# Turning the first half's mirrored tiles by scattered accumulation, one flip matmul for the rest, late residuals summed by transfers, and taps behind the warm-up, in a gated mix of a long convolution and an MLP

## Chip, cores, metric

One core of one Trainium2 chip. The metric is device time in microseconds (us) of one launch, median of several launches. A run counts as slow when it is over 1.5% above the fastest of the same kernel. A ratio is the mean time of one kernel's fast runs over the mean of the other's fast runs of the same rounds, so it is not quite the ratio of the medians that are quoted. Spans and starts are those of the one profiled launch of each kernel; that of the kernel before (245.66 us, granted clock 0.99) is slow, so no difference of some tenths of a us against it is read as an effect.

## The reference, cut to what matters

Shapes: 2048 rows (16 tiles of 128), D = 640, F = 1536, bfloat16.

```python
def reference(A_q, A_k, A_v, A_shift_k, A_ssm_k, A_ssm_D, B_x, B_w1, B_w2, B_w3, B_w4, gate_w):
    x = A_q
    g = sigmoid((x * gate_w).sum(-1))
    # A: 4-tap shift of k, times v, causal convolution with ssm_k over 2048 rows (by FFT), plus D, times q
    kv = (sum over 4 taps of shifted k * shift_k) * v
    y = irfft(rfft(kv, 4096) * rfft(ssm_k, 4096))[:2048] + kv * ssm_D
    a = x * y
    # B: layer norm, w1, gelu, shifts of four groups, w2, residual; layer norm, w3, gelu, w4, residual
    x1 = x + shifted(gelu(layernorm(x) @ w1)) @ w2
    b = x1 + gelu(layernorm(x1) @ w3) @ w4
    return g * a + (1 - g) * b
```

## The kernel before: what the change and the argument touch

The kernel records operations (`P.op`, `P.dma`); a list scheduler with tuned biases fixes one order for each engine, and every engine runs its list in that order. The convolution is made of transforms folded at 1024 rows: 16 final steps (k = 0 to 15; 0 to 7 are columns 0 to 319, the "first half") each turn one spectrum into two tiles of 128 rows, `ts_` and `td`. The two inverse transforms `ab[0]`, `ab[1]` give tile `ts_` as their sum and tile `td` as their difference with the rows in reverse. The reversal ("flip") is a matmul with a reversed identity. Both results are multiplied with gated rows of q and accumulated onto the output by a transfer from GpSimd (k < 12), or added to the residual and stored.

```python
    for i in range(WARM):                        # 12 pairs of warm-up matmuls
        P.op("pe", [warm-up matmul] * 2, ...)
    ...
    for c in range(DC):                          # 5 tap matmuls; the schedule puts them among the warm-ups
        pr = ps(1, "set")
        mm(pr, [(Esel[:, 128 * c:128 * (c + 1)], shk5)])
        act(SHK[:, ::-1, 128 * c:128 * (c + 1)], pr..., ACTF.Copy)

    def pool_pow(o, a, e, dur=900):              # layer norms: x ** -0.5 on GpSimd, 128 x 1 or 128 x 2 elements
        P.op("pool", lambda g: g.tensor_tensor(o, a, e, ALU.pow), [a, e], [o], dur)

    def mm4(t):                                  # w4; the residual of the second half by an identity matmul
        for h in range(2):
            mm(pr[:, h, :], [... w4 ...] + ([] if summed(h, t) else [(ident, X[:, t, hs])]))
        act(X[:, t, :]..., pr, ACTF.Copy, scale=gst[4][:, t:t + 1])
        P.dma("pool", o, x, accum=True)

    def unit(hh, c):                             # products of spectra on VectorE
        def prod(o, a, r):
            tt(v3(o), XF[:, hh, c - a], h, ALU.mult)       # 128 x 2560 as two of 1280, both inputs in SBUF
        # ... cut

    def final(hh, c, q, k):
        qt, gy, ab = qb[k], gyb[k % 8], (abb[k % 4] if k < 12 else abl[k - 12])
        P.dma(sp, qt, rows(A_q))
        act(qt[:, 0], qt[:, 0], ACTF.Copy, scale=gst[3][:, ts_:ts_ + 1])
        # ... two inverse transforms into pr
        act(ab, pr, ACTF.Copy)
        tt(gy[:, 0], ab[:, 0], ab[:, 1], ALU.add)
        mm(pf, [(flip, ab[:, 0]), (negflip, ab[:, 1])])
        act(gy[:, 1], pf, ACTF.Copy, scale=gst[3][:, td:td + 1])
        tt(gy, gy, qt, ALU.mult)                 # k >= 14: in two parts
        # k < 12: P.dma("pool", rows(out), gy, accum=True);  k >= 12: add X, store by SyncE
```

## Time and profile before

| kernel before | |
|---|---|
| time, median of 3 runs | 245.17 us (242.52 to 246.2) |
| profiled span | 243.6 us (slow) |
| busy: TensorE / VectorE / GpSimd | 228.8 / 216.6 / 95.3 us |
| matmuls; GpSimd instructions | 1486; 120 |
| TensorE's last unbroken stretch ends | 234.96 us |
| from there to the end (below: the tail) | 8.6 us |

The prediction shows the lines. In them PE is TensorE (PEld its weight loads), DVE VectorE, ACT ScalarE, POOL GpSimd and SP SyncE; SBUF and PSUM are the two on-chip memories, and matmuls write to PSUM. Only one more of the kernel before is needed later: the longest GpSimd instruction (apart from the closing drain) is a power operation of 2.0 us.

### The profile page before, as it was taken

Reading aid. Unit: us, or ns where it says so; the run is one execution under the profiler, and the core shown is the slowest. Engines: PE = TensorE matmul, PEld = TensorE weight load, DVE = VectorE, ACT = ScalarE, POOL = GpSimd, SP = SyncE. Lnnn points to the kernel's source line nnn. Section 1 sums busy time; section 2 is a strip of 40 time slices with the busy share of each in tenths; the row PEclk is TensorE's granted clock in tenths of the full one; section 3 lists DMA queues with packets and bytes.
Section 4 is the critical chain, followed back from the end, with each engine's and each line's share of the span. In section 5 each row is a group of like instructions: output and inputs, shape, how many; then the busy total and the mean of one; then the engine's idle time right before and its main releaser. Section 6 shows DMA issues by size and latency. Waiting matters only on the chain.

```text
span 243.6 us, 4130 instructions
## 1 busy us (share of the span) xinstructions
PE 228.8 (94%) x1486; PEld 136.9 (56%) x1486; DVE 216.6 (89%) x384; ACT 171.2 (70%) x317; POOL 95.3 (39%) x120
## 2 busy tenths in 40 slices
PE   6998998999997999999999999999999999999970
PEld 1276775544643654555577545775557754677640
DVE  5859999999988999999998569999999999997382
ACT  2456797888775999999375996337895466228980
POOL 0235524970272470530246321335105375323761
PEclk9999999999999999999999999999999999999996
DMA  6999599899699999489747963399987989997997
GB/s 179 348 344 341 156 224 158 202 210 241 156 189 181 295 261 269 127 202 335 206 68 152 168 164 81 64 149 193 200 208 113 164 95 169 171 176 129 128 125 137
DMA packets 65304, 45.53 MB, mean 187 GB/s; under 512 B 28930, under 2 KB 60548, under 8 KB 65284
## 3 DMA queue, kind: packets, MB, share of 16 engines
q1 hardware_dynamic: 56268, 33.36, 53.9%
q0 software_dynamic: 8832, 11.80, 33.1%
q8 instruction: 11, 0.18, 0.3%
q10 hardware_dynamic: 184, 0.11, 0.3%
q14 instruction: 9, 0.07, 0.1%
HBM read 24.29 MB, written 6.55 MB: 127 GB/s over the span
## 4 chain that ended last, share of the span: by engine, by line
PE 70%; DVE 15%; DMA 7%; POOL 3%; issue 2%; ACT 1%; DVEq 0%
PE PSall L1246 65%; DVE arena L1226 8%; DMA arena<-in_B_w_dram 4%; PE PSall L1272 4%; DMA arena<-arena 2%; POOL arena L1231 2%; DVE arena L1479 2%; DVE arena L1231 2%; DVE arena L1412 2%; ACT arena L1236 1%; POOL arena L1416 1%; DVE arena L1413 0%; PE PSall L1457 0%; DVE arena L1514 0%; DVE arena L1268 0%
## 5 line engine op out<-in xcount | busy, mean ns | idle before, releaser
L1246 PE MATMUL PSall<-arena 128*128 128x320 bf16 (+4 forms) x1420 | 217.2, 312 | 5.7 <-ACT arena L1236 2.9
L1226 DVE TENSOR_TENSOR arena<-arena 128x640 bf16<-128x640 bf16 (+5 forms) x231 | 178.5, 824 | 12.0 <-ACT arena L1236 10.7
L1246 PEld LDWEIGHTS PSall<-arena 128*128 128x128 bf16 (+1 forms) x1420 | 131.1, 98 | 90.9 <-ACT arena L1236 6.5
L1236 ACT ACTIVATE arena<-PSall 128x512 bf16<-128x512 f32 (+4 forms) x181 | 109.3, 674 | 26.6 <-PE PSall L1246 22.4
L1236 ACT ACTIVATE arena<-arena 128x640 bf16<-128x640 bf16 (+3 forms) x70 | 45.8, 692 | 12.1 <-DVE arena L1226 8.8
L240 POOL DMA_DIRECT2D out_dram<-arena x28 | 29.3, 1112 | 32.9 <-ACT arena L1236 25.6
L1231 POOL TENSOR_SCALAR arena<-arena 128x1 f32<-128x1 f32 (+2 forms) x41 | 24.7, 610 | 39.1 <-ACT arena L1236 14.2
L1236 ACT ACTIVATE arena<-PSall,arena 128x640 bf16<-128x640 f32 (+1 forms) x32 | 20.8, 660 | 25.6 <-PE PSall L1246 25.3
L1416 POOL TENSOR_TENSOR arena<-arena 128x1 f32<-128x1 f32 (+1 forms) x24 | 20.6, 877 | 44.4 <-DVE arena L1231 43.9
L240 POOL DMA_DIRECT2D arena<-arena x12 | 14.9, 1238 | 26.2 <-DVE arena L1226 25.7
L1231 DVE TENSOR_SCALAR arena<-arena 128x640 bf16<-128x640 bf16 (+3 forms) x47 | 14.3, 317 | 3.0 <-ACT arena L1236 1.4
L1412 DVE BATCH_NORM_STATS2 arena<-arena 128x6 f32<-128x320 bf16 x32 | 13.9, 476 | 2.5 <-DMA arena<-in_A_q_dram 2.4
L1272 PE MATMUL PSall<-arena 128*128 128x512 bf16 x24 | 9.7, 566 | 2.3 <-DVE arena L1268 2.3
L1479 DVE TENSOR_SCALAR arena<-arena 32x256 bf16<-32x256 bf16 (+1 forms) x24 | 5.8, 243 | 3.6 <-ACT arena L1236 3.2
L1226 POOL TENSOR_TENSOR arena<-arena 128x1 f32<-128x1 f32 (+1 forms) x11 | 7.7, 734 | 0.4
L1272 PEld LDWEIGHTS PSall<-arena 128*128 128x128 bf16 x24 | 2.8, 128 | 7.8 <-issue 5.0
L1514 DVE SCALAR_TENSOR_TENSOR arena<-PSall,arena 128x640 bf16<-128x640 f32 x8 | 6.5, 813 | 0.1
L1236 ACT ACTIVATE PSall<-PSall 128x640 f32<-128x640 f32 x8 | 5.6, 703 | 0.1
L1457 PE MATMUL PSall<-arena 128*128 128x128 bf16 x40 | 3.5, 241 | 0.0
L1457 PEld LDWEIGHTS PSall<-arena 128*128 128x128 bf16 x40 | 3.1, 111 | 0.6 <-DVE arena L1412 0.3
L1275 ACT ACT_TABLE_LOAD x1 | 1.3, 1283 | 2.2 <-issue 2.2
L1413 DVE BATCH_NORM_AGGREGATE arena<-arena 128x2 f32<-128x12 f32 x16 | 2.8, 196 | 0.0
(24 smaller groups left out, 9.9 us busy)
## 6 DMA issues: line engine op xcount, KB each, us to landing
arena<-arena POOLq DMA_DIRECT2D x12, 640.0 KB, 6.3
arena<-in_A_k_dram SPq DMA_DIRECT2D x14, 400.0 KB, 4.4
arena<-in_A_q_dram SPq DMA_DIRECT2D x20, 160.0 KB, 3.9
out_dram<-arena POOLq DMA_DIRECT2D x20, 160.0 KB, 4.1
arena<-in_A_v_dram SPq DMA_DIRECT2D x16, 160.0 KB, 4.4
arena<-in_A_ssm_k_dram SPq DMA_DIRECT2D x5, 512.0 KB, 5.1
arena<-in_A_q_dram SPq DMA_DIRECT2D x6, 320.0 KB, 6.5
arena<-in_B_w_dram SPq DMA_DIRECT2D x1, 1920.0 KB, 10.7
```

The costliest lines, as they stand in the source:

```text
L240: fn = lambda e: e.dma_start(out, in_, **kw)
L1226: P.op(eng, lambda e: e.tensor_tensor(o, real(a), real(b), op), [a, b], [o], dve_ns(o, [a, b], 2) if eng == "dve" else 500)
L1231: P.op(eng, lambda e: e.tensor_scalar(o, real(a), s1, s2, op0=op0, **({} if op1 is None else {"op1": op1})), [a] + aps, [o], dve_ns(o, [a] ...
L1236: P.op("act", lambda e: e.activation(real(o), real(a), f, bias=bias, scale=scale, **({"accum_out": accum} if accum is not None else {})), ...
L1246: fns.append(lambda e, l=l, r=r, i=i: e.matmul(real(o), l, r, start=(i == 0), stop=(i == last)))
L1272: P.op("pe", [lambda e: e.matmul(real(pw), warm[:, 0:128], warm[:, 128:640], start=True, stop=True)] * 2, [warm], [pw], 856.0 if i < 5 els ...
L1412: P.op("dve", lambda e, o=o, i=i: e.bn_stats(o, i), [i], [o], 400)
L1413: P.op("dve", lambda e: e.bn_aggr(bna[:, t, :], bns[k]), [bns[k]], [bna[:, t, :]], 120)
L1416: P.op("pool", lambda g: g.tensor_tensor(o, a, e, ALU.pow), [a, e], [o], dur)
L1457: P.op("pe", [lambda e, c=c, pb=pb, xn=xn: e.transpose(real(pb)[:, 128 * c:128 * (c + 1)], xn[:, 128 * c:128 * (c + 1)], ident) for c in r ...
L1479: P.op("dve", lambda e, o=hT[q, 4, c0:c0 + n], i=hx[q, :]: e.tensor_scalar(o, i, 1.0, None, op0=ALU.mult), [hx[q, :]], [hT[q, 4, c0:c0 + n ...
L1514: P.op("dve", lambda e: e.scalar_tensor_tensor(x, real(pr), 1.0, x, op0=ALU.mult, op1=ALU.add, accum_out=st[1, 0][:, t:t + 1]), [pr, x], [ ...
```

## The change

Its intent is to take work from TensorE. First-half steps: no flip; the second tile's rows of q are loaded in reverse order by an indirect transfer (a gather), and the product is accumulated in reverse order by another (a scatter-add). Second-half steps: VectorE subtracts, so that one flip matmul does. The residual of tiles 0 to 7 in the second half goes by an accumulating transfer within SBUF, not by a matmul. The taps wait for the warm-up's last matmul. All scheduler biases (over 1,300 numbers) are new, so the order of nearly everything moves.

```diff
@@ taps
-        mm(pr, [(Esel[:, 128 * c:128 * (c + 1)], shk5)])
+        o = mm(pr, [(Esel[:, 128 * c:128 * (c + 1)], shk5)])
+        o.preds.setdefault(warmed.idx, False)
@@ mm4 (cut)
-            mm(pr[:, h, :], [... w4 ...] + ([] if summed(h, t) else [(ident, X[:, t, hs])]))
-        act(X[:, t, :].rearrange("p (b n) -> p b n", b=2), pr, ACTF.Copy, scale=gst[4][:, t:t + 1])
+            mm(pr[:, h, :], [... w4 ...])
+        away = None if summed(1, t) else V(oW2 + 320 * t, 320)
+        act(dst, pr, ACTF.Copy, scale=gst[4][:, t:t + 1])
         P.dma("pool", o, x, accum=True)
+        if away is not None:
+            P.dma("pool", X[:, t, 320:640], away, accum=True)
@@ final
-        P.dma(sp, qt, rows(A_q))
+        turn = k < TURNED                                        # TURNED = 8
+        if turn:
+            P.dma(sp, qt[:, 0], rows(A_q)[:, 0])
+            P.dma("pool", qt[:, 1], rows(A_q)[:, 1], fn=lambda e: e.indirect_dma_start(qt[:, 1], None, q320, rev, **at))
+            act(qt[:, 1], qt[:, 1], ACTF.Copy, scale=gst[5][:, td:td + 1])
+        else:
+            P.dma(sp, qt, rows(A_q))
@@
+        if turn:
+            tt(gy[:, 1], ab[:, 0], ab[:, 1], ALU.subtract)
+            tt(gy, gy, qt, ALU.mult)
+            P.dma("pool", rows(out)[:, 0], gy[:, 0], accum=True)
+            P.dma("pool", rows(out)[:, 1], gy[:, 1], accum=True,
+                  fn=lambda e: e.indirect_dma_start(out320, rev, gy[:, 1], None, compute_op=ALU.add, **at))
+            return
-        mm(pf, [(flip, ab[:, 0]), (negflip, ab[:, 1])])
+        tt(ab[:, 0], ab[:, 0], ab[:, 1], ALU.subtract)
+        mm(pf, [(flip, ab[:, 0])])
@@ cut: new biases, the scheduler's estimate of an indirect transfer, base tiles of 640 columns, the turned gate
```

## The prediction

> **What bounds the kernel now.** I read the engine totals, then the chain that ended last, then busy time in stretches of 10 us, then the start and the end in order of time. Totals and chain on the page:
>
> ```profile
> PE 228.8 (94%) x1486; PEld 136.9 (56%) x1486; DVE 216.6 (89%) x384; ACT 171.2 (70%) x317; POOL 95.3 (39%) x120
> PE 70%; DVE 15%; DMA 7%; POOL 3%; issue 2%; ACT 1%; DVEq 0%
> ```
>
> TensorE and VectorE are both nearly full; the chain in order of time says which counts where:
>
> ```profile
> 108.39 10.69 DMA arena<-in_B_w_dram
> 119.08 0.14 issue
> 119.21 113.31 PE PSall L1246 x729
> ```
>
> From 119.2 to 232.5 us it is TensorE without a break. It starts when w4 lands, 0.15 us after TensorE ran out of other work. Before that the chain lies on VectorE from about 18 to 47 us, then mostly on TensorE. Stretches (columns: stretch, then PE, PEld, DVE, ACT, POOL busy with counts, clock, DMA share, GB/s):
>
> ```profile
> 10.00:20.00 10.00, 9.13 (x64) 6.11 (x63) 6.98 (x25) 4.41 (x9) 1.95 (x4) 1.00 1.10 329
> 20.00:30.00 10.00, 9.80 (x105) 7.57 (x103) 9.88 (x27) 7.35 (x20) 6.14 (x9) 1.00 0.72 234
> 130.00:140.00 10.00, 10.00 (x64) 6.04 (x63) 6.97 (x11) 7.53 (x13) 5.26 (x8) 1.00 0.92 153
> 140.00:150.00 10.00, 10.00 (x50) 4.74 (x49) 8.14 (x8) 9.99 (x18) 2.81 (x2) 1.00 0.49 126
> 150.00:160.00 10.00, 10.00 (x75) 7.01 (x74) 10.00 (x10) 3.61 (x7) 2.98 (x3) 1.00 0.48 92
> ```
>
> VectorE is full from 20 us, loses 4.9 us between 130 and 150, and is full again until 220. It is a close second: a saving on TensorE is worth only what VectorE can follow. The start in order of time (start, us, engine, line, operation, count, idle before):
>
> ```profile
> 9.13 0.13 PEld L1272 LDWEIGHTS PSall<-arena 128*128 128x128 bf16 x2 [0.84 <-issue]
> 9.13 3.59 PE L1272 MATMUL PSall<-arena 128*128 128x512 bf16 x8
> 13.58 1.46 PE L1272 MATMUL PSall<-arena 128*128 128x512 bf16 x6
> 14.87 2.89 PE L1246 MATMUL PSall<-arena 128*128 128x256 bf16 x25
> 18.22 0.92 DVE L1479 TENSOR_SCALAR arena<-arena 32x256 bf16<-32x256 bf16 x4 [2.71 <-ACT arena L1236]
> ```
>
> The warm-up matmuls (L1272) still take some 430 ns each at 9 us and about 216 ns (half) only after 12.5 us, since the tap matmuls stand among them with gaps of up to 0.84 us. The first real matmuls (14.87) queue behind them, and VectorE idles 2.71 us for their result. The end:
>
> ```profile
> 221.77 13.18 PE L1246 MATMUL PSall<-arena 128*128 128x320 bf16 x95
> 221.81 1.55 DVE L1226 TENSOR_TENSOR arena<-arena 128x1280 bf16<-128x1280 bf16 x2
> 233.83 5.05 DVE L1226 TENSOR_TENSOR arena<-arena 128x320 bf16<-128x320 bf16 x17 [0.23 <-ACT arena L1236]
> ```
>
> VectorE hands over the last product of the second half at 223.4 us. TensorE reaches the matmuls that read it at about 229, so VectorE has some 5 us in hand. Then evictions and VectorE's last operations run to 238.9, and the last stores land by 243.6.
>
> **What the Trainium skill says.** "TensorE: Matmul & The Clock Gate", Part 1 (the clock gate): the clock is half until TensorE has been busy for about 3.4 us, whatever the number of matmuls, and a warm matmul starts every N/2.4 GHz plus 2.5 ns. The trace agrees: 13.18 us / 95 = 138.7 ns for 320 columns, and the clock doubled only after the unbroken run of 3.4 us from 9.1. "DMA: Bandwidth & Descriptors", SWDGE vs HWDGE: accumulating transfers can be issued from GpSimd only; here its 28 accumulations into the output took 1.112 us of POOL each. "SBUF — State Buffer", Who interferes with whom: a VectorE operation with two SBUF inputs contends with GpSimd instructions that read SBUF. No view here separates that; if it bites, more GpSimd transfers slow VectorE.
>
> **The change part by part.** Rows I take costs from:
>
> ```profile
> L1226 DVE TENSOR_TENSOR arena<-arena 128x320 bf16<-128x320 bf16 x24 | 6.9, 319 | 3.6 <-ACT arena L1236 3.5
> L1236 ACT ACTIVATE arena<-PSall,arena 128x320 bf16<-128x320 f32 x16 | 8.2, 528 | 2.8 <-PE PSall L1246 2.5
> L1236 ACT ACTIVATE arena<-arena 128x320 bf16<-128x320 bf16 x24 | 13.6, 597 | 0.0
> L1236 ACT ACTIVATE arena<-arena 128x640 bf16<-128x640 bf16 x24 | 20.3, 882 | 2.5 <-DMA arena<-arena 2.5
> ```
>
> *TensorE.* The 16 final steps had two flip matmuls each; now eight have none and eight one: 24 fewer. The second-half residual of tiles 0 to 7 no longer goes through an identity matmul: 8 fewer. 32 x 138.7 ns = 4.4 us, nearly all in the stretch where TensorE is the chain. A gate flip adds two tiny matmuls.
>
> *Start.* The taps go behind 20 unbroken warm-up matmuls. If the clock doubles at about 7.4 us (my estimate: one to two windows of 3.4 us after 2.3), 12 run at 430 and 8 at 216 ns and end near 9.1; transposes, evictions (0.7 us each), four warm-ups and two taps then put the first real matmul at about 11.3 instead of 14.9. TensorE gains 3.5 us, but from 18 to 47 us VectorE is the chain, so the end gains only its idle time: 2.7 us.
>
> *VectorE.* Each final step gets one more subtraction of 128x320 (before, the negated flip did it): 16 x 0.319 = 5.1 us. By the new order some 7 of the eight first-half ones, and all three operations of one first-half step that used to come later, stand before the last second-half product: 7 x 0.32 + 1.1 = 3.3 us. Against it the starting gain, 2.7, and most of the 4.9 us idle: in the new order the transform matmuls it waited for come ahead of the w4 stage, and products fill the rest; I take 4. Last product at 223.4 + 3.3 - 2.7 - 4 = 220.
>
> *ScalarE.* Eight flip evictions of 0.528 become eight scalings of turned rows (0.597): +0.6 us. Eight base tiles grow from 320 to 640 columns: 8 x 0.285 = 2.3 us, where ScalarE has some room.
>
> *GpSimd and transfers.* 40 transfers become 64 (eight gathers, eight scatter-adds in place of half of eight stores, eight sums within SBUF). The indirect ones have no row here; I assume 1.2 to 1.9 us of POOL. 48 plain ones at about 1.0 to 1.2 plus 16 of these are some 70 to 85 us, within about 115: room in sum, queues in places. Bytes hardly change.
>
> *Sum.* TensorE reaches the second-half final steps at 224 - 2.7 - 2.8 (20 of its 32 savings lie before) = 218.5, and the steps that read the last product at about 222.5, just after VectorE's 220 plus an eviction. The tail then is ScalarE's and VectorE's: eight double evictions of 0.71, eight flip evictions of 0.53, and VectorE with eight more subtractions: 6 steps x 1.4 + 2 x 1.7 + 1.1 = 12.9 us from 220, so about 233 to 234, and 4.7 us to the last landing: about 238. By the other count, 243.6 - 2.7 - 4.4 + 0.6 (a subtraction now stands ahead of each flip) + about 1 for w4 (below) = 238.1. So 5.5 us less; on the median, 245.2 - 5.5 = 239.7.
>
> **Rivals.** *VectorE becomes the bound.* For: full from 150 to 220, 5.1 us of work added. Against: idle time before and after. If the stretch at 130 to 150 keeps its idle, the last product comes at 224 and the time is about 242 to 243. *w4 comes late.* In the new order the last reader of the region w4 overwrites comes late: between it and w4's first use stand 30 matmuls of 512 and 25 of 320 columns, 30 x 0.216 + 25 x 0.139 = 9.9 us, against 10.7 us of loading. For: today it is met within 0.15 us. Against: the load waited in a busy stretch. 1 to 3 us; I count 1. *GpSimd's queue is in order.* A transfer waiting for its data holds the product sums behind it, which VectorE needs: 1 to 4 us in the worst case, 241 to 243. *The start is no gain,* since transfers (share 1.10, 329 GB/s) feed VectorE too late: 242.
>
> **Range and chances.** The middle is 239.7. All rivals together give about 244, none with a better reordering 236.5. Runs of one kernel spread by 3.7 us (242.5 to 246.2), plausibly as the clock's window falls differently. So 236.5 to 243.5. The 2% line is 240.3, next to the middle; parts that only help slightly outweigh: faster 0.55, same 0.41, slower 0.04.
>
> **What would show it.** Right: warm-up matmuls at half their time from 6 to 9 us; first 128x256 matmul at 10.5 to 12; VectorE's 2.7 us wait gone; 1,456 matmuls, TensorE busy 6 to 9 us less; VectorE busy about 221.7; the chain still TensorE for most. Wrong: VectorE waits for POOL transfers in the product stage, TensorE idle over 2 us ahead of w4's first use, indirect issues above 3 us, VectorE's 128x2560 products slower than their 1.483 us, or a tail after TensorE's last matmul longer than 8 us (now 6.8).

## The result, and the profile after

The changed kernel took **254.09 us** (median of 4 runs, 252.76 to 255.24) against 244.79 us of the kernel before in the same rounds: ratio 1.041, 95% interval 1.031 to 1.051. It is slower; 239.7 had been predicted, at most 243.5.

Totals and chain of the page after (they answer to the first two lines of the prediction):

```profile
PE 225.4 (89%) x1444; PEld 133.1 (53%) x1456; DVE 220.8 (87%) x400; ACT 174.0 (69%) x318; POOL 141.4 (56%) x146
PE 31%; DVE 25%; ACT 15%; DMA 14%; POOL 6%; issue 5%; SPq 3%; POOLq 0%
```

The instruction counts came out as worked out (1,456 weight loads; twelve matmul records are missing from the trace). TensorE does less, but the chain is on it for 31% of the span instead of 70%: it waits. GpSimd has 46 us more. Busy time in stretches (columns as in the prediction), first of the kernel before, then of the changed one:

```profile
170.00:180.00 10.00, 10.00 (x56) 5.23 (x54) 10.00 (x16) 8.81 (x19) 1.10 (x2) 1.00 1.10 221
```

```profile
170.00:180.00 10.00, 5.90 (x29) 2.63 (x27) 7.47 (x12) 3.71 (x7) 9.70 (x3) 1.00 0.33 80
180.00:190.00 10.00, 8.87 (x34) 4.33 (x35) 5.27 (x7) 7.96 (x16) 7.45 (x7) 0.66 0.49 93
```

TensorE, VectorE and ScalarE all drop there, the granted clock falls to 0.66 afterwards, and GpSimd is 97% busy with three instructions. The same stretch in order of time, changed kernel, for GpSimd, VectorE, ScalarE and TensorE (start, us, engine, line, operation, count, idle before):

```profile
163.48 1.00 POOL L1640 DMA_INDIRECT arena<-in_A_q_dram,arena  x1 [0.30 <-issue]
...
167.11 11.30 POOL L1640 DMA_INDIRECT arena<-in_A_q_dram,arena  x1 [0.30 <-issue]
...
159.31 18.17 DVE L1233 TENSOR_TENSOR arena<-arena 128x2560 bf16<-128x2560 bf16 x23
...
180.03 0.56 ACT L1243 ACTIVATE arena<-arena 128x320 bf16<-128x320 bf16 x1 [5.60 <-DMA arena<-in_A_q_dram,arena]
...
181.13 4.18 PE L1253 MATMUL PSall<-arena 128*128 128x512 bf16 x12 [5.18 <-ACT arena L1243]
```

One gather took 11.30 us of GpSimd where another took 1.00. It lies beside 18.17 us of VectorE operations without a gap and ends within a microsecond of VectorE running dry (177.48). ScalarE, which runs in order, waits 5.60 us for its rows; TensorE waits 5.18 us for ScalarE.

The second loss is at the end. First the kernel before, then the changed one, TensorE in order of time:

```profile
223.81 11.15 PE L1246 MATMUL PSall<-arena 128*128 128x320 bf16 x80
235.80 0.99 PE L1246 MATMUL PSall<-arena 128*128 128x320 bf16 x6 [0.85 <-ACT arena L1236]
```

```profile
223.82 16.46 PE L1253 MATMUL PSall<-arena 128*128 128x320 bf16 x120
245.19 0.71 PE L1253 MATMUL PSall<-arena 128*128 128x320 bf16 x2 [4.90 <-DVE arena L1233]
```

The last two flips wait 4.90 us for VectorE, where six matmuls waited 0.85 us for ScalarE. The tail grows from 8.6 us (234.96 to 243.6) to 13.1 us (240.29 to 253.4).

### The profile page after: what moved, and what is told of

Its sections match the earlier page's. It is cut to its first block, busy times and chain, and to the rows that moved or that the text cites.

```text
span 253.4 us, 4110 instructions
## 1 busy us (share of the span) xinstructions
PE 225.4 (89%) x1444; PEld 133.1 (53%) x1456; DVE 220.8 (87%) x400; ACT 174.0 (69%) x318; POOL 141.4 (56%) x146
## 4 chain that ended last, share of the span: by engine, by line
PE 31%; DVE 25%; ACT 15%; DMA 14%; POOL 6%; issue 5%; SPq 3%; POOLq 0%
PE PSall L1253 31%; DVE arena L1233 18%; ACT arena L1243 15%; DMA arena<-arena 6%; DMA arena<-in_A_q_dram,arena 5%; DMA arena<-in_A_q_dram 3%; SPq L242 3%; POOL arena L1425 2%; DVE arena L1421 2%; DVE arena L1238 2%; POOL arena L242 2%; DVE arena L1488 1%; POOL arena L1238 1%; POOL arena L1640 1%; DVE arena L1422 0%
## 5 line engine op out<-in xcount | busy, mean ns | idle before, releaser
L1233 DVE TENSOR_TENSOR arena<-arena 128x2560 bf16<-128x2560 bf16 (+4 forms) x247 | 183.1, 794 | 17.3 <-ACT arena L1243 16.1
L1253 PEld LDWEIGHTS PSall<-arena 128*128 128x128 bf16 (+1 forms) x1390 | 128.0, 98 | 104.9 <-ACT arena L1243 16.3
L1243 ACT ACTIVATE arena<-arena 128x640 bf16<-128x640 bf16 (+3 forms) x78 | 51.3, 683 | 18.4 <-DMA arena<-in_A_q_dram,arena 6.0
L1238 POOL TENSOR_SCALAR arena<-arena 128x1 f32<-128x1 f32 (+3 forms) x42 | 27.6, 658 | 41.3 <-ACT arena L1243 20.6
L1243 ACT ACTIVATE arena<-PSall,arena 128x640 bf16<-128x640 f32 (+1 forms) x24 | 16.1, 704 | 23.2 <-PE PSall L1253 23.2
L242 POOL DMA_DIRECT2D arena<-arena x20 | 23.5, 1256 | 13.5 <-DVE arena L1233 10.8
L1640 POOL DMA_INDIRECT arena<-in_A_q_dram,arena x8 | 20.2, 2520 | 2.4 <-issue 2.4
L1656 POOL DMA_INDIRECT out_dram<-arena x8 | 14.5, 1811 | 3.5 <-issue 1.5
L1279 PE MATMUL PSall<-arena 128*128 128x512 bf16 x24 | 7.4, 473 | 2.2 <-DVE arena L1275 2.2
L1233 POOL TENSOR_TENSOR arena<-arena 128x1 f32<-128x1 f32 (+2 forms) x12 | 5.6, 468 | 6.7 <-DVE arena L1238 6.0
```

Of the source, the lines that this page charges most:

```text
L242: fn = lambda e: e.dma_start(out, in_, **kw)
L1233: P.op(eng, lambda e: e.tensor_tensor(o, real(a), real(b), op), [a, b], [o], dve_ns(o, [a, b], 2) if eng == "dve" else 500)
L1238: P.op(eng, lambda e: e.tensor_scalar(o, real(a), s1, s2, op0=op0, **({} if op1 is None else {"op1": op1})), [a] + aps, [o], dve_ns(o, [a] ...
L1243: P.op("act", lambda e: e.activation(real(o), real(a), f, bias=bias, scale=scale, **({"accum_out": accum} if accum is not None else {})), ...
L1253: fns.append(lambda e, l=l, r=r, i=i: e.matmul(real(o), l, r, start=(i == 0), stop=(i == last)))
L1279: warmed = P.op("pe", [lambda e: e.matmul(real(pw), warm[:, 0:128], warm[:, 128:640], start=True, stop=True)] * 2, [warm], [pw], 856.0 if ...
```

## The experiments

Each table row is a run of the whole kernel; medians are of all its runs, ratios of the fast ones against the kernel before. "Holds us" is the longest GpSimd instruction apart from the closing drain.

| run | median us | ratio, 95% | profiled span | holds us | tail us |
|---|---|---|---|---|---|
| changed kernel | 254.09 | 1.041 (1.031 to 1.051) | 253.4 | 11.30 | 13.1 |
| plain_gather | 255.17 | 1.041 (1.030 to 1.053) | 256.2 (slow) | 7.68 | |
| plain_both | 252.94 | 1.035 (1.022 to 1.048) | 252.4 | 7.67 | 13.0 |
| drain | 257.09 | 1.053 (1.045 to 1.062) | 254.2 | 7.67 | 13.4 |
| pow_gap | 247.89 | 1.016 (1.007 to 1.025) | 245.7 | 2.20 | 13.4 |
| gaps | 252.14 | 1.034 (1.028 to 1.040) | 251.3 | 2.48 | 13.2 |
| old_flip | 253.47 | 1.027 (1.016 to 1.038) | 251.7 (slow) | 6.27 | |
| gaps_flip | 251.33 | 1.032 (1.025 to 1.038) | 249.5 | 2.59 | 12.7 |
| few_gaps | 250.24 | 1.023 (1.017 to 1.029) | 248.4 | 2.59 | 14.2 |
| tail_single | 257.88 | 1.059 (1.052 to 1.066) | 255.5 | 2.50 | 25.1 |
| tail_flip | 252.92 | 1.037 (1.029 to 1.044) | 250.7 | 2.89 | 14.5 |
| taps_only | 243.39 | 0.996 (0.993 to 0.999) | 242.1 | 2.32 | 8.7 |
| half_turned | 253.26 | 1.032 (1.026 to 1.038) | 252.1 | 2.88 | 16.1 |
| half_former | 247.36 | 1.012 (1.009 to 1.016) | 245.3 | 2.87 | 9.0 |
| half_none | 249.24 | 1.010 (1.001 to 1.020) | 256.4 (slow) | 12.96 | |
| half_one | 246.36 | 1.010 (1.006 to 1.014) | 243.2 | 2.87 | 9.6 |

### First series: is it the gather?

**plain_gather** and **plain_both**: the indirect load, then also the scatter-add, become plain transfers of the same bytes, rows in forward order (values wrong). The order of all engines is unchanged.

```diff
-            P.dma("pool", qt[:, 1], ..., fn=lambda e: e.indirect_dma_start(qt[:, 1], None, q320, rev, **at))
+            P.dma("pool", qt[:, 1], ..., fn=lambda e: e.dma_start(qt[:, 1], fwd(A_q)))
 # plain_both also:
-                  fn=lambda e: e.indirect_dma_start(out320, rev, gy[:, 1], None, compute_op=ALU.add, **at))
+                  fn=lambda e: e.dma_start(fwd(out), gy[:, 1], accum_op=ALU.add, max_dma_last_dim=4096))
```

> The changed kernel, same order on every engine, but the eight turned loads are plain GpSimd loads of the same rows in forward order, so no index is read (results of eight half tiles wrong on purpose). Theory 1 (starved gather: the indirect load must read its indices from SBUF and cannot while VectorE runs an unbroken series of operations with two SBUF inputs): no load issue above 2 us, no TensorE stall at 172 to 186 us, time 241 to 245 us instead of 254. Theory 2 (GpSimd's queue is simply too full with 64 transfers instead of 40): the queue still holds 64, time 250 us or more.

> As the kernel with plain loads, and the eight scatter-adds are plain accumulating stores too (wrong on purpose in the same half tiles). Theory 1: within 1.5 us of the kernel with plain loads alone, because the scatter-adds (1.6 to 2.6 us of GpSimd each) have nobody waiting for them. Theory 2: a clear further gain, 3 us or more.

Both stayed near the changed kernel. plain_gather's time is one that theory 2 had expected too; pow_gap below, with the same 64 transfers, speaks against it. So the gather as such was not the cause: with it gone, another GpSimd instruction was held, a power operation of the layer norm on 128x1 elements. Duration (min/median/max in ns) of these operations, kernel before and plain_both:

```profile
L1416 POOL TENSOR_TENSOR arena<-arena x24: 544/726/2012, 7.1 to 144.5; 128x1 f32<-128x1 f32 x16, 128x2 f32<-128x2 f32 x8
```

```profile
L1425 POOL TENSOR_TENSOR arena<-arena x24: 547/847/7673, 6.7 to 142.5; 128x1 f32<-128x1 f32 x16, 128x2 f32<-128x2 f32 x8
```

The held one, and the same operation at the same place of the changed kernel:

```profile
127.62 7.67 POOL L1425 TENSOR_TENSOR arena<-arena 128x1 f32<-128x1 f32 x1
```

```profile
127.66 1.99 POOL L1425 TENSOR_TENSOR arena<-arena 128x1 f32<-128x1 f32 x1
```

So an unbroken VectorE series can hold a GpSimd instruction but need not: VectorE's operations beside these two are the same, and without a gap until 134.9 in both. Of the six profiled kernels without added gaps there, five hold this operation (7.7 us in plain_gather, plain_both and drain, 6.3 in old_flip and half_none), and the changed kernel does not.

**drain**: the changed kernel, VectorE operations in the gathers' stretch waiting each for its own predecessor.

```diff
+    for a, b in zip(vec, vec[1:]):               # vec: VectorE's operations in order
+        if lo <= b.order <= hi and b.grp.startswith(("unit", "final")):
+            b.preds[a.idx] = True
```

> The changed kernel, correct results, with one addition: from just before the first turned load to the last one, each VectorE operation of the product and final steps waits for the one before it to finish, so its series has gaps. Theory 1: the third turned load takes under 3 us instead of 11.3, the stall is gone, and the time falls to 243 to 248 us although VectorE pays some 0.1 us for each of about 45 waits. Theory 2: no load gets shorter, and the time rises by the waits, to 255 to 259 us.

No gather took over 2.11 us any more, but a power operation ahead of that stretch took 7.67 us, and the time rose by 3.0 us: theory 1 was right on the gather and wrong on the time.

**gather_probe**: the three kinds of transfer by themselves, 81,920 bytes each, alone and beside series of 12 VectorE operations of one kind.

```python
    vec series: "two" = tensor_tensor 128x2560, both inputs in SBUF; "chain" = the same, each waiting for the one before;
                "one" = one SBUF input; "psum" = one input in PSUM
    one GpSimd transfer ("gather", "plain", "scatter") is released after the first operation of the series
```

> Not the kernel: a probe (output meaningless on purpose). First gather, plain accumulating store and scatter-add on GpSimd with VectorE idle, twice. Then series of 12 VectorE operations, with one transfer issued when the first of them is done: 128x2560 additions with two SBUF inputs (about 1.4 us each) with a gather, again with a plain store, again with a scatter-add; the same additions each waiting for the one before, with a gather, and with a scatter-add; one-input multiplications with a gather; additions with one PSUM input with a gather, and with a scatter-add. Theory 1: 1.0 us for a gather alone; about 15 us, to the end of the series, beside the unbroken two-input series; 1 to 1.5 us for the plain store; under 3 us where each addition waits; about 1 us beside PSUM additions. Theory 2: 1 to 2 us everywhere.

GpSimd in order of time; the first two (a plain one between them took 0.95 us) are alone, the last three beside the two-input series:

```profile
16.88 1.09 POOL L43 DMA_INDIRECT gat<-in_A_q_dram,ix  x1 [16.42 <-DMA out_dram<-sb]
...
22.90 1.61 POOL L45 DMA_INDIRECT out_dram<-sb,ix  x1 [2.04 <-DMA out_dram<-sb]
...
38.46 2.02 POOL L43 DMA_INDIRECT gat<-in_A_q_dram,ix  x1 [3.69 <-DVE sb L36]
55.42 0.95 POOL L44 DMA_DIRECT2D out_dram<-sb  x1 [14.95 <-DVE sb L36]
72.36 2.61 POOL L45 DMA_INDIRECT out_dram<-sb,ix  x1 [15.98 <-DVE sb L36]
```

An indirect transfer needs about 1.0 us longer beside such a series, a plain accumulating one (0.95 us) does not notice it. Beside VectorE operations with one input in PSUM the gather took 0.96 us, the scatter-add 1.59 us, as alone. So two-input operations do get in the way, but the probe shows a delay of 1.0 us, about two thirds of one operation (1.49 us), not the 15 us that theory 1 expected of it, nor the 7 to 11 us of the kernels. Nor did gaps help in the probe: beside additions that each wait for the one before, the gather took 2.15 us and the scatter-add 2.71. The theory was widened: any GpSimd instruction that reads SBUF (gather, scatter-add, power operation) can be held until VectorE makes a gap. The runs below bear out that gaps prevent the holds, but not that only a gap ends one.

### Second series: gaps, and the flips

**pow_gap**: plain_both with the self-waits around the last layer norms only, 20 operations.

```diff
+    for a, b in zip(vec, vec[1:]):
+        if lo <= b.order <= hi:                  # from the last kv products to just past the last layer norm
+            b.preds[a.idx] = True
```

> The plain_both kernel (252.9 us; its longest POOL instruction was a power operation of the second layer norm, 7.67 us, with TensorE idle for 5.9 us behind it), with one change: 20 of VectorE's operations around the last layer norms wait for their own predecessor, which makes a gap of some 34 ns each. Theory 1, widened: a GpSimd instruction that reads SBUF can be held by an unbroken series of VectorE operations with two SBUF inputs until the first gap; so no power operation takes over 3 us, the idle time of TensorE at 133 to 139 us is gone, and the time is 245 to 249 us. Rival: the power operation waits for something else that comes at that moment (a transfer, ScalarE): it still takes over 6 us and the time stays at 251 to 254.

247.89 us, 5.1 less than plain_both. VectorE's series of eight operations beside the held one in plain_both; then the power operations of pow_gap, and the same series there:

```profile
126.31 10.09 DVE L1233 TENSOR_TENSOR arena<-arena 128x2560 bf16<-128x2560 bf16 x8
```

```profile
L1425 POOL TENSOR_TENSOR arena<-arena x24: 547/856/1885, 7.1 to 138.3; 128x1 f32<-128x1 f32 x16, 128x2 f32<-128x2 f32 x8
```

```profile
126.06 10.84 DVE L1233 TENSOR_TENSOR arena<-arena 128x2560 bf16<-128x2560 bf16 x8
```

The longest power operation fell from 7.67 to 1.89 us, and TensorE's wait behind it from 5.85 to 0.99 us. The price is in the last lines: 0.75 us for some seven gaps more, about 0.11 us each. In the trace one operation otherwise starts some 86 ns before the one ahead of it ends; a self-wait makes 34 ns between them. In plain_both the held operation began at 127.62, VectorE's first gap (35 ns) came at 134.87, and it ended at 135.29, 0.42 us after the end of a VectorE operation. A gap is not needed for that: in old_flip and half_none the same operation ended 0.42 to 0.43 us after the end of a VectorE operation too (134.87 and 133.56), about 1 us ahead of the next gap.

**gaps** (the changed kernel, every second VectorE operation from there to the end of the first half, some 60 gaps), **old_flip** (the second half's steps with the former two flip matmuls, in the same order of all else) and **gaps_flip** (both):

```diff
 # old_flip
-        tt(ab[:, 0], ab[:, 0], ab[:, 1], ALU.subtract)
-        mm(pf, [(flip, ab[:, 0])])
+        mm(pf, [(flip, ab[:, 0]), (negflip, ab[:, 1])])
```

> The changed kernel, with right results, every second VectorE operation from the last kv products to the last first-half final step waiting for its predecessor (some 60 gaps of some 34 ns, so about 2 us more on VectorE). Widened theory 1: no POOL instruction over 3.5 us outside the end, TensorE idle between 130 and 190 us down by 5 us, 246 to 250 us; the idle time ahead of the last two flips stays near 4.9 us. Rival (what costs the time is the new order of the work, not held GpSimd instructions): 253 us or more.

> The changed kernel in the same order, except that the eight second-half final steps use the two former flip matmuls (flip and negated flip) and no subtraction on VectorE: 8 matmuls of 0.139 us more, 8 operations of 0.32 us fewer. Theory 2 (the flips wait for a subtraction that stands late in VectorE's in-order queue): TensorE's idle time ahead of the last two flips goes from 4.9 to under 1.5 us, from the last inverse matmul to VectorE's last operation it is 3 to 4 us instead of 7.2, and the time falls by 3 to 5 us, to 249 to 251. Rival (VectorE's load at the end is what counts, not the place of the subtraction): 1 to 2 us less. The held GpSimd instruction stays, since nothing ahead of the last steps is changed.

> Both of the above in one: gaps on VectorE and the two former flip matmuls in the second half. If the two causes are separate and together the whole loss: the sum of both gains, 242 to 246 us, at or a little below the kernel before; start gain kept. If over 249, a third cause is still to be found.

gaps removed the holds and gained only 2 us: 60 gaps at 0.11 us are some 6 us of VectorE (an estimate from pow_gap), and its chain of waits now lies mostly on VectorE from 140 to 223 us. old_flip is inconclusive in time: four of its six runs lie at 253 to 254 us and count as slow, and its ratio rests on the two fast ones. In its trace, of a slow run, TensorE's wait ahead of the last flips is gone, as expected, and still the tail is 12.1 us; in gaps_flip, a fast run, it is 12.7 us, and the time is 0.8 us below gaps. So theory 2 in its simple form (the flips wait for the subtraction, and this is the tail) fell: VectorE and the last transfers fill the same time.

### Third series: fewer gaps, the former end, and the taps alone

**few_gaps**: the changed kernel with 34 gaps, at the next and the third next VectorE operation behind each GpSimd instruction that reads SBUF.

```diff
+    for p in held:                               # power operations, gathers, scatter-adds
+        if lo <= p.order <= hi:
+            marks.update([n for n, o in enumerate(vec) if n and o.order > p.order][:3:2])
+    for n in marks:
+        vec[n].preds[vec[n - 1].idx] = True
```

> The changed kernel (254.1 us), right results, with some 30 VectorE gaps in place of the 60 of the gaps run: only the next VectorE operation and the third next after each GpSimd instruction that reads SBUF (power operations of the layer norm, gathers, scatter-adds) waits for its own predecessor. Theory 1, widened (a GpSimd instruction that reads SBUF is held until VectorE's next gap): no POOL instruction over 5 us, TensorE's idle stretch of 5 to 6 us gone, and since half the gaps cost half, 249 to 251 us, under the 252.1 of the gaps run. If the gap's place does not matter or the loss is elsewhere: 252 or more.

250.24 us: right results, 3.9 us less than the changed kernel. TensorE's last unbroken stretch now ends at 234.17, ahead of the kernel before (234.96). What is left of the loss stands behind it.

**tail_single** and **tail_flip**: few_gaps with the last operations of all engines in the former order, the second also with the former flips.

```diff
+    sched = P.schedule(quota, forced=(first part as it was, last part by the positions in the former order))
```

> few_gaps, and the operations from the last transform steps on put in the order in which the kernel before has them (flips among the inverse matmuls, each subtraction just ahead of its flip) instead of all flips after all inverse matmuls. The single flips with their subtraction stay. Theory 3 (the tail is long because of its order: VectorE idles 3.8 us, then runs its last 20 operations in a row after the last flips): from TensorE's last inverse matmul to the end 9 to 11 us instead of 13, and 2 to 3 us less than few_gaps. Rival theory 2 (the subtraction itself makes the tail long, wherever it stands): less than 1 us gained.

> tail_single, with the two former flip matmuls in place of subtraction and single flip in the second half. Theory 3: 0.5 to 1.5 us less than tail_single (8 VectorE operations of 0.32 us fewer), tail 8.5 to 10 us as in the kernel before, some 245 to 247 us in all. Theory 2: 3 to 5 us less than tail_single.

Theory 3 (only the order makes the tail long) fell as well: both are slower than few_gaps. Their traces say why. VectorE of tail_single, then ScalarE of tail_flip:

```profile
237.53 2.18 DVE L1242 TENSOR_TENSOR arena<-arena 128x320 bf16<-128x320 bf16 x7 [7.51 <-DMA out_dram<-arena]
```

```profile
240.43 1.78 ACT L1252 ACTIVATE arena<-PSall,arena 128x320 bf16<-128x320 f32 x4 [3.47 <-DMA out_dram<-arena]
```

They wait for transfers **into the output**: step 8 may write its buffer only when step 0's product has been stored from it. Step 0's data was ready 60 us earlier, but its tiles' w4 result must be accumulated first, and that comes last. The Trainium skill, "DMA: Bandwidth & Descriptors", Rules for kernel authors, says that an accumulating transfer must wait for an earlier one on the same bytes; the kernels all do, and no run here drops that wait. So this store stands near the end of GpSimd's queue, behind those of steps 1, 6 and 7, and the change made two transfers of each. GpSimd of tail_flip (steps 7 and 0):

```profile
232.10 1.54 POOL L242 DMA_DIRECT2D out_dram<-arena  x1
233.94 1.61 POOL L1667 DMA_INDIRECT out_dram<-arena  x1 [0.30 <-issue]
234.97 1.53 POOL L242 DMA_DIRECT2D out_dram<-arena  x1
236.80 1.68 POOL L1667 DMA_INDIRECT out_dram<-arena  x1 [0.30 <-issue]
```

No idle time is left between them but that of issuing. Whether step 0's two transfers could have gone ahead of those of steps 6 and 7 was not tried. In the former kernel the second tile's flip read `ab` alone; in tail_single the subtraction overwrites `ab` and so has to follow the sum, which needs the buffer: that is why it is the slowest of all.

**taps_only**: the kernel before in its own order, only the taps behind the warm-up.

```diff
+        o.preds.setdefault(warmed.idx, False)    # each tap matmul
```

> The kernel before in its own order, with nothing changed but the five tap matmuls, which go behind the warm-up matmuls as in the change. The start's gain of the prediction by itself: first real matmul at about 11 us instead of 14.9, VectorE's wait of 2.7 us gone, and 2 to 3 us less at the end (ratio 0.988 to 0.992). If transfers or VectorE take it back later: within 0.5 us of the kernel before.

243.39 us, ratio 0.996 (0.993 to 0.999), 22 runs: the only version that beats both kernels, by 1.0 us of the 2.7 predicted. TensorE of the kernel before and of taps_only around 75 us:

```profile
77.89 2.39 PE L1246 MATMUL PSall<-arena 128*128 128x1 bf16 x31 [1.09 <-ACT arena L1236]
```

```profile
75.74 6.51 PE L1252 MATMUL PSall<-arena 128*128 128x1 bf16 x52 [1.95 <-ACT arena L1242]
```

Before these waits taps_only led by 3.0 us (the same two matmuls end at 73.79 against 76.81), behind them by 2.15 (75.74 against 77.89): its TensorE waits 1.95 us for ScalarE, which waited 2.38 us for a transfer within SBUF, where the kernel before waits 1.09. The profiled span ends 1.5 us ahead, of a slow run of the kernel before; where the rest went was not followed.

### Fourth series: turn only where GpSimd's queue has room

**half_turned**: few_gaps, only steps 2 to 5 turned; steps 0, 1, 6 and 7, whose stores come last, with two flip matmuls and one transfer. **half_former**: also the former flips in the second half, and the former order of the end.

```diff
-    TURNED = 8
-        turn = k < TURNED
+        turn = k in (2, 3, 4, 5)
```

> few_gaps (250.2 us), but only the first-half steps 2 to 5 are turned; steps 0, 1, 6 and 7, whose stores come last, have the two former flip matmuls and one accumulating transfer for both tiles. The second half keeps single flips with their subtraction. 8 matmuls of 0.139 us more, 4 transfers fewer and 4 scatter-adds of 1.6 us become plain in the last 30 us. Theory 4 (GpSimd's queue at the end): GpSimd has pauses in the last 20 us, no eviction waits for a transfer into the output, and 2 to 4 us are gained: 246 to 248 us. If the order (subtractions and flips last) alone makes the tail: 249.5 to 251.

> half_turned with the former two flip matmuls in the second half and the former order of the end. With theory 4 and the held instructions as the whole of the loss: from TensorE's last unbroken stretch to the end 8.5 to 9.5 us as in the kernel before (8.6), 243 to 246 us in all, within 0.5% of the kernel before. If something else lengthens the tail: 248 or more.

half_turned missed: 253.26, not 246 to 248. In the scheduler's order (all flips after all inverse matmuls) its tail is 16.1 us, so fewer transfers in the queue alone did not shorten it. half_former hit its tail, 9.0 us, and came to 247.36; its time was expected at 243 to 246, so 1.4 us were missed. The cleanest pair is tail_flip against half_former: both have the former flips and the former end, and differ in four turned steps (and, with these, in ten gaps, some 1.1 us of VectorE). The tail is 14.5 against 9.0 us, 5.5 us shorter, and the time 252.92 - 247.36 = 5.6 us. ScalarE of half_former at the place where tail_flip's waited 3.47 us:

```profile
236.98 2.02 ACT L1253 ACTIVATE arena<-PSall,arena 128x320 bf16<-128x320 f32 x4
```

**half_none** and **half_one**: half_former with no gap, and with 14 of its 24; the order on every engine is the same.

```diff
-            marks.update([...][:3:2])
+            marks.update([...][:0])              # half_one: [:1]
```

> half_former (247.4 us) without any of the added VectorE gaps; the order on all engines is the same. Theory 1, widened: a GpSimd instruction that reads SBUF is held again for over 5 us, TensorE idles 4 to 6 us behind it, and the time is 250 to 253 us although VectorE saves the 2.6 us of the gaps. If the gaps did nothing but cost: 244.5 to 246 us.

> half_former with only one gap for each GpSimd instruction that reads SBUF (the next VectorE operation), 14 in all instead of 24. If one gap is enough to let the instruction in and the rest of the loss is the gaps' own cost: no POOL instruction over 4 us and about 1 us less, 246 to 247 us. If one is not enough: a held instruction of over 5 us and 249 us or more.

Without gaps the holds are back. GpSimd of half_none (two places, its slowest run) and of half_one (the second place):

```profile
127.29 6.27 POOL L1435 TENSOR_TENSOR arena<-arena 128x1 f32<-128x1 f32 x1
...
189.61 12.96 POOL L1671 DMA_INDIRECT out_dram<-arena  x1 [0.30 <-issue]
```

```profile
184.69 2.87 POOL L1671 DMA_INDIRECT out_dram<-arena  x1 [0.30 <-issue]
```

half_none's five runs spread from 245.86 to 258.26 us, half_one's 22 from 243.88 to 248.32. By the three fast runs alone half_none (1.010) is no slower than half_former (1.012), where 250 to 253 us was expected: in time this pair shows nothing. That the spread comes from holds that differ from run to run is likely, but only the profiled run, a slow one, shows its holds; the claim that gaps end the holds does not rest on it: of the changed kernel, plain_both and drain, all profiled in fast runs without gaps at the place of the hold, each has one of 7.7 to 11.3 us, and none of the nine kernels with gaps there has a GpSimd instruction over 2.9 us. 14 waits did as well as 24 in half_one's profiled run. That one gap is what lets an instruction in is not shown: none falls inside the 2.87 us of the line above (the nearest are at 184.54 and 190.67). half_one's median is 1.0 us below half_former's, near the 1.1 us that ten gaps cost by the estimate; by the ratios it is 0.6 us, within the noise.

## Why the prediction was wrong, point by point

1. **TensorE, 32 matmuls fewer.** The count was right, and TensorE's busy time fell (228.8 to 225.4 us, in few_gaps 222.9), though not by the 6 to 9 us of the sign. That it is "nearly all in the stretch where TensorE is the chain" was wrong: with the holds gone VectorE holds 38% of few_gaps' chain and TensorE 20%. Rival 1, VectorE as the bound, came true once the larger losses were out.
2. **Start, 2.7 us.** The mechanism was right (warm-ups unbroken from 2.24 to 8.61, first real matmul at 10.8), the size was not: 1.0 us at the end in taps_only, as a later wait took some of it back. The reading of the clock was loose: the "gaps of up to 0.84 us" are those of the weight loads (the line is of PEld), while the longest pause in the starts of the 512-column matmuls there was some 0.14 us beyond their 0.43. Nor did 3.6 us of unbroken warm-ups from 2.29 us speed up those at 7.2 us in the kernel before; in the changed kernel the clock doubled 3.8 us after the start, at 6.05.
3. **VectorE: "products fill the rest; I take 4".** This is the step that failed. VectorE did fill its idle time: 9.97 of 10 us busy from 140 to 150 against 8.14. But with VectorE's pauses gone, GpSimd's power operations and gathers could be held: beside the former pauses (0.5 to 1.8 us long between 129 and 142 us) no power operation of the kernel before took over 2.0 us, and beside the new series five of six profiled kernels held one for 6.3 to 7.7 us, and the sixth, the changed kernel itself, held a gather for 11.3. The prediction quoted the Trainium skill, "SBUF — State Buffer", Who interferes with whom, on the contention, and then took it in one direction only: "more GpSimd transfers slow VectorE". It went the other way: VectorE's unbroken series held GpSimd, ScalarE waited in order, TensorE waited 4 to 6 us. VectorE's own products were not slower (1.49 us on average against 1.48). The sign was in the list ("indirect issues above 3 us"), not in the sum. Gaps alone take 3.9 us off (few_gaps), after paying for themselves.
4. **GpSimd: "room in sum, queues in places".** The sum was right and did not matter. Where the queue matters, at the end, the change put two transfers of 0.9 and 1.6 us for one of 1.2 behind the last w4 results, and second-half steps wait for the buffers these free. Rival 3 named the in-order queue, for the product sums, and gave it 1 to 4 us; in the former order of the end it is 5.5 us of tail (tail_flip against half_former).
5. **Tail: "+0.6 (a subtraction now stands ahead of each flip)".** The tail is 4.5 us longer in the changed kernel (8.6 to 13.1 us). The prediction's own sign, over 8 us behind the very last matmul, did not show it (7.5 us), since the loss stands ahead of that matmul. A subtraction is 0.32 us, but it stands in VectorE's queue behind the products of other steps, and overwrites what the sum must read first. The wait ahead of the last flips is 4.90 us. Removing the subtraction alone gained nothing that the runs could show, since the queue of point 4 fills the same time; the former flips, the former order and the queue's relief together give 9.0 us.
6. **w4 late, 1 us.** Not seen; TensorE does not pause ahead of w4's first use (121.8 us).

Still open: why, beside the same unbroken series, two gathers took 2.0 and 1.0 us and the third 11.3 us, and one power operation took 1.99 us in one kernel and 7.67 in another; why the probe shows a delay of 1.0 us only, and no help from gaps; and what the last 1.0% of half_one over the kernel before (some 2.4 us by the fast runs) is made of (14 gaps cost some 1.5 us by the estimate above, and VectorE also does the four turned steps' subtractions).

## What to carry to other kernels

Idle time of an engine can be what another engine lives on: before filling VectorE with two-input SBUF operations, look which GpSimd instructions read SBUF beside it, and who waits for them in order; in these kernels a wait of some VectorE operations for their own predecessor (about 0.11 us each) placed beside them kept every hold away, though why it does so is not settled. Count a queue's room not over the whole span but behind the last event that its entries wait for, and follow which buffers those entries free. A model that makes a step cheaper on one engine by splitting its store should be asked what the split does where stores pile up.

## What the Trainium skill lacked or had wrong

- "SBUF — State Buffer", Who interferes with whom: right that two-input VectorE operations contend with GpSimd reads (gather 1.09 to 2.02 us, scatter-add 1.61 to 2.61 us in the probe) and that one SBUF input and one in PSUM do not (0.96 us). Lacking: how long such a contention can last. The one length it gives, the whole instruction, is said of the two-port modes; here GpSimd instructions were held 5.5 to 13.0 us, over several VectorE operations, and one beside the like series of another run was not held (1.99 us).
- The same section says that a software-issued transfer is stalled through descriptor generation, while two-input operations take only the read interface. Here plain accumulating transfers indeed took 0.95 us either way, but indirect ones, whose row numbers lie in SBUF, took 1.0 us longer beside two-input operations.
- No page read for this case gives the GpSimd time of an indirect transfer: 1.0 to 1.1 us for a gather and 1.6 us for a scatter-add of 128 rows of 640 bytes, against 0.95 us for a plain accumulating one.
- "VectorE: DVE Perf Modes", The DRAIN you can't avoid, finds that a semaphore after each of eight copies costs nothing extra. Lacking: a price for two-input operations that wait each for its own predecessor, which is about 0.11 us here (the overlap of some 86 ns lost, and 34 ns between).
